# QK-normed attention and a layer-normed MLP on one core: first attention reordered, preparation moved between ScalarE, VectorE and GpSimd

## The chip, the cores and the metric

One core of one Trainium2 chip runs the whole kernel. The metric is the time of one execution in microseconds (us), as the device reports it; lower is better. The engines are TensorE (PE, with its weight loads shown as PEld), VectorE (DVE), ScalarE (ACT), GpSimd (POOL) and SyncE (SP, which here only issues DMAs). A line such as L789 is a line of the kernel before.

## The reference

Inputs are `q`, `k`, `v` of shape (8 batches, 12 heads, 448 positions, 64), the gains `g_q`, `g_k` (64), `g_ln` (768), and the MLP weights `w_ch1` (768 x 3072) and `w_ch2` (3072 x 768). All are float32, and so is the output (8, 448, 768).

```python
def rmsnorm(x, g):
    rms = np.sqrt(np.mean(x * x, axis=-1, keepdims=True) + 1e-06)
    return x / rms * g
q_n, k_n = rmsnorm(q, g_q), rmsnorm(k, g_k)
attn = softmax(q_n @ k_n.T / sqrt(64))          # over the keys
x = (attn @ v), heads side by side              # (8, 448, 768)
xn = (x - mean) / sqrt(var + 1e-06) * g_ln
out = x + relu(xn @ w_ch1) @ w_ch2
```

## The kernel before

**Units and pairs.** The 12 heads of a batch are 6 pairs, so there are 48 pairs, numbered 0 to 47. Loading and normalizing is done by units (`UNITS`, L22): batch 0 has units 0 and 1 with one pair each and units 2 and 3 with two pairs each (pairs 2, 3 and 4, 5); each later batch has three units of two pairs, so unit 4 is pairs 6 and 7, unit 5 is 8 and 9, unit 6 is 10 and 11, unit 7 is 12 and 13, unit 8 is 14 and 15. A pair has seven tiles of 128 keys: six of its own heads and one (i = 6) that takes the last 64 keys of both heads.

**Preparing a unit** is a set of small steps, each with a letter (`pieces`, L229 to L347). `b` takes the tiles. `a` and `c` square keys and queries (L257, ACT), `d` and `e` sum the squares over 64 columns (L260, DVE), `g` (or `gq`, `gk`) takes the reciprocal roots (L263, L264, ACT). `i` multiplies the keys by both gains (L274), `j` rounds them to 16 bits, the high part (L280 POOL or L282 ACT), `k` subtracts to get the low part (L285, DVE). `l` scales the queries (L82, DVE), `m` duplicates them beside the low and high keys (L321). `z` copies the values to 16 bits (L327, L333, POOL). The squares are written where the 16-bit tiles (`khl`, `qn`) will stand, so a high part waits for the sum that reads the squares. Which engine does a step for which unit is set by lists: `DVE_KG` for `i`, `POOL_HI` for `j`, `POOL_DUP` for `m`, and `ACT_Q`, by pair, for the copy of the transposed queries.

**Transposing.** Up to unit 6, PE transposes keys and queries pair by pair: `K` (`trans_k`, L363 and L366, copied out by DVE at L368) and `Q` (`trans_q`, L377 and L380, copied out by ACT at L383 or by DVE at L385). From unit 7 on (`DMA_UNIT`), SP issues transposing DMAs: steps `x` (keys, L301), `y` (queries, L307) and `Y` (the last 64 queries, the "left" ones, L313).

**Attention.** `S p.i` is the score product of a tile and its exponential: PE at L400 (or L406, L410, L411 for the seventh tile), then ACT at L416 with the key's norm as scale. `V p.i` multiplies the exponentials with the values (L453, L455); after the seventh, DVE evacuates the pair, divided by the sum (L468 to L475). Two PSUM banks take scores.

**MLP.** `T` takes statistics of finished pairs (L635, DVE), `A` aggregates them (L650), `N` normalizes a tile of 128 positions (L656), `X` transposes it (for batch 0 with PE at L692, copied by ACT at L696 and L698 or by DVE at L700; for later batches with SP's transposing DMAs, L682), `R` takes the root. For batch 0, `U` does the first three column blocks of the up product tile by tile (L936), then `first_mlp` does the other 21 blocks (L712, rectified by ACT at L715) and the down products (L722, added by DVE at L749). Later batches go by `mlp_group`, which forms the down product from seven block products in place of eight; its sums of weights (`weight_sums`, L755) are made by DVE near the end of batch 0's MLP.

**What sets the order.** Every engine works through its own instructions in the order in which they are written down. Up to the start of batch 0's MLP that order is the list `ORDER`, written out by hand: S, V, K, Q, T and the steps named above, with the unit or pair behind the letter. `H` and `J` are filler products and filler transposes on PE, so many as the number says. `L` loads a unit, `W` a third of the first weight matrix (POOL's queue), `G` and `G2` load and scale the layer norm's gain. Afterwards `attention` makes a list of steps for all later pairs, seven per pair, with what falls due at each: `EARLY` spreads the steps of units 5 to 9, `TRANS_AT` sets the steps for `x`, `y`, `Y`, `W2_AT` those for the second weight matrix (L610, POOL's queue; the second time POOL first waits for unit 7's transposed keys, L607). A step that stands in `ORDER` already is left out. `run_rest` mixes this list into the MLP of the batch before: after each chunk of MLP work it takes as many steps as its share. `TAIL` is the number of pieces of 960 ns of MLP work that are to be left when the steps are through; after that the norm of the next batch follows, one item per chunk.

**Loads.** SP issues most loads. Keys and queries of units have a ring of three buffers (`p_in`, tag "kq"); `RING` is the order in which they get them, and a buffer is loaded again when its low part (`k`) or scaled queries (`l`) are done. Some loads have a home of their own (`home`, L192) in memory that isn't yet in use: `hS`, which later takes the MLP's activations, and `free`, which later takes sums of weights.

## Time and profile before

| | |
|---|---|
| Median of 3 runs | 588.28 us (586.68 to 588.32) |
| The profiled execution | 588.25 us |
| Its span in the trace, first to last instruction | 586.6 us |
| Around the span | 1.65 us |
| Granted TensorE clock, mean | 0.999 |

Times in a trace are counted from the span's start. In the views, a row of a stretch of time gives start, duration, engine, line, operation, what it writes and reads, how many instructions were merged, and in brackets how long the engine had been idle before and who ended that. "SPq" and "POOLq" are the queues of the engines that issue DMAs. A time at which a row starts serves as its name in the text.

### The profile page before, as it was taken

What the parts mean: (1) busy time and instruction counts of PE and PEld (TensorE: products, weight loads), DVE (VectorE), ACT (ScalarE), POOL (GpSimd) and SP (SyncE); (2) the same over time, 40 slices, a digit from 0 to 9 for tenths busy, and PEclk for the clock granted to TensorE, in tenths of its full rate; (3) what the DMA queues carried; (4) which work ended last, traced back from release to release, by engine and by line L of the source; (5) the groups of instructions that cost most, each with busy time, mean ns of one, the idle gap of its engine ahead of it and who ended that gap; (6) DMA issues with size and microseconds to landing.
All of it is one profiled execution on the core that took longest, in us unless ns stands there. A gap on an engine that the chain in (4) does not pass through costs nothing.

```text
span 586.6 us, 13638 instructions
## 1 busy us (share of the span) xinstructions
PE 561.6 (96%) x5438; PEld 412.5 (70%) x5438; DVE 378.3 (64%) x831; ACT 378.9 (65%) x693; POOL 178.8 (30%) x200
## 2 busy tenths in 40 slices
PE   6777999999999999999999999999999999999996
PEld 5555566667677867777687767777777777777784
DVE  5898666697667586855757576864756733663424
ACT  5987888448785688647787488737787477323130
POOL 2945335303240520653141511643241410020000
PEclk9999999999999999999999999999999999999999
DMA  8999999969762786968753697959743490040201
GB/s 215 262 217 230 187 185 180 176 157 137 127 113 49 180 125 146 121 159 106 138 92 56 178 131 142 126 143 119 145 62 65 123 105 1 1 108 2 83 1 56
DMA packets 178328, 72.58 MB, mean 124 GB/s; under 512 B 138212, under 2 KB 173220, under 8 KB 178260
## 3 DMA queue, kind: packets, MB, share of 16 engines
q1 hardware_dynamic: 133876, 52.52, 44.0%
q0 software_dynamic: 43440, 18.52, 25.7%
q8 instruction: 43, 0.70, 0.5%
q10 hardware_dynamic: 944, 0.62, 0.5%
q14 instruction: 25, 0.20, 0.1%
HBM read 52.76 MB, written 11.01 MB: 109 GB/s over the span
## 4 chain that ended last, share of the span: by engine, by line
PE 77%; DVE 7%; ACT 3%; DMA 3%; issue 1%; SPq 1%; DVEq 0%; ACTq 0%
PE psH L789 32%; PE psP L812 27%; PE psS L400 7%; PE oA L453 4%; PE psH L712 3%; DMA q<-in_q_dram 2%; PE oB L455 1%; ACT E L416 1%; PE psS L406 1%; DVE stat L635 1%; DVE w2s L755 1%; DVE ssq L260 1%; ACT khl L257 1%; DVE xn L656 1%; DVE x L470 1%
## 5 line engine op out<-in xcount | busy, mean ns | idle before, releaser
L416 ACT ACTIVATE E<-psS,rr_all 128x448 f16<-128x448 f32 x336 | 203.7, 635 | 39.4 <-PE psS L400 33.7
L789 PE MATMUL psH<-xnT,w 128*128 128x256 f16 (+1 forms) x2016 | 225.8, 261 | 1.3 <-DVE x L749 1.3
L789 PEld LDWEIGHTS <-w 128*128 128x128 f16 x2016 | 172.6, 98 | 25.5 <-issue 6.4
L792 ACT ACTIVATE hS<-psH 128x512 f16<-128x512 f32 x150 | 90.1, 601 | 98.4 <-PE psH L789 94.0
L812 PEld LDWEIGHTS <-hS 128*128 128x128 f16 x1080 | 100.0, 98 | 57.5 <-issue 1.1
L812 PE MATMUL psP<-w,hS 128*128 128x384 f16 x672 | 126.8, 326 | 0.0
L400 PE MATMUL psS<-qU,kU 128*128 128x448 f16 x288 | 100.9, 352 | 7.3 <-ACT E L416 4.5
L453 PEld LDWEIGHTS <-E 128*128 128x128 f16 x1008 | 70.5, 98 | 35.6 <-issue 3.7
L274 POOL TENSOR_TENSOR k<-k,gprod 128x896 f32<-128x896 f32 x19 | 40.5, 2132 | 158.2 <-ACT khl L257 131.8
L795 DVE TENSOR_TENSOR hS<-hS 128x512 f16<-128x512 f16 (+1 forms) x119 | 56.8, 484 | 22.3 <-ACT hS L792 20.8
L812 PE MATMUL psP<-w2s,hS 128*128 128x384 f16 (+1 forms) x408 | 69.9, 321 | 0.0
L453 PE MATMUL oA<-v,E 128*128 128x65 f16 x864 | 66.4, 193 | 1.0 <-POOL v L327 0.6
L749 DVE SCALAR_TENSOR_TENSOR x<-psP,rs_all,x 128x384 f32<-128x384 f32 x60 | 36.4, 617 | 41.9 <-PE psP L812 41.2
L455 PE MATMUL oB<-v,E 128*128 128x65 f16 x288 | 51.7, 193 | 0.2
L823 POOL TENSOR_TENSOR x<-x,hS 128x384 f32<-128x384 f32 x21 | 23.5, 1128 | 83.5 <-ACT hS L891 82.9
L215 POOL DMA_DIRECT2D v<-in_v_dram x54 | 41.4, 777 | 9.0 <-PE oB L455 8.0
L468 DVE RECIPROCAL rec_all<-oA 128x6 f32<-128x6 f32 x48 | 9.2, 192 | 47.5 <-PE oA L453 47.4
L285 DVE TENSOR_TENSOR khl<-k,khl 128x896 f16<-128x896 f32 x19 | 20.8, 1094 | 29.3 <-ACT khl L282 29.2
L400 PEld LDWEIGHTS <-kU 128*128 128x128 f16 x288 | 28.0, 98 | 14.5 <-issue 3.5
L891 ACT ACTIVATE hS<-hS,rs_all 128x384 f32<-128x384 f32 x27 | 14.6, 605 | 33.1 <-DVE hS L795 33.1
L455 PEld LDWEIGHTS <-E 128*128 128x128 f16 x336 | 32.4, 97 | 0.2 <-DVE xl L475 0.2
L260 DVE TENSOR_REDUCE ssq<-khl 128x14 f32<-128x896 f32 (+1 forms) x24 | 25.5, 1063 | 10.1 <-ACT khl L257 9.2
(141 smaller groups left out, 610.0 us busy)
## 6 DMA issues: line engine op xcount, KB each, us to landing
k<-in_k_dram SPq DMA_DIRECT2D x19, 384.0 KB, 3.8
q<-in_q_dram SPq DMA_DIRECT2D x19, 384.0 KB, 4.3
out_dram<-x SPq DMA_DIRECT2D x14, 384.0 KB, 2.9
w<-in_moe_w_ch_dram POOLq DMA_DIRECT2D x3, 1536.0 KB, 15.7
v<-in_v_dram POOLq DMA_DIRECT2D x54, 64.0 KB, 4.6
out_dram<-x POOLq DMA_DIRECT2D x9, 384.0 KB, 2.7
w<-in_moe_w_ch_dram POOLq DMA_DIRECT2D x1, 2304.0 KB, 22.4
w<-in_moe_w_ch_dram POOLq DMA_DIRECT2D x2, 1152.0 KB, 14.3
```

The costliest lines, as they stand in the source:

```text
L215: nc.gpsimd.dma_start(out[:, :, j, 0:D], main[:, :, j])
L260: nc.vector.tensor_reduce(out=c["ssq"][:, n], in_=c["sq", n], axis=AX.X, op=ALU.add)
L274: (nc.vector if u in DVE_KG else nc.gpsimd).tensor_tensor(out=c["t"][1], in0=c["t"][1], in1=sh.gprod.unsqueeze(1).broadcast_to([128, g, D] ...
L400: nc.tensor.matmul(ps[0][:, 0:S], c["main"][:, ts(i, 128)], c["q"][:, ts(h, S)], start=True, stop=True)
L416: nc.scalar.activation(out=o, in_=x[:, 0:S], func=AFT.Exp, scale=self.units[u][3][:, g:g + 1], bias=EXP_BIAS)
L453: nc.tensor.matmul(oA[:, t, cs], E[:, ts(t, 128)], rhs, start=(i == 0 and t == 0), stop=(i == 6 and t == 2))
L455: nc.tensor.matmul(oB[:, cs], E[:, 320:448], rhs, start=(i == 0), stop=(i == 6))
L749: self.nc.vector.scalar_tensor_tensor(out=x, in0=ps, scalar=self.rs[:, b, t:t + 1], in1=x, op0=ALU.mult, op1=ALU.add)
L789: nc.tensor.matmul(ps[:, i], sh.w1[:, dc, ts(f + i, 128)], self.xnT[:, dc, 256 - N:256], start=(i == 0 and dc == 0), stop=(i == k - 1 and ...
L792: nc.scalar.activation(out=hT[:, f:f + k], in_=ps, func=AFT.Relu)
L795: nc.vector.tensor_tensor(out=out, in0=a, in1=c, op=op)
L812: nc.tensor.matmul(bank[x][:, c], a[:, f], w[:, f, c], start=(start and f == 0), stop=(stop and f == HALF - 1))
```

## The change

It has these parts.

1. **`ORDER`** is another permutation. It now holds `b`, `a`, `c`, `d`, `e` and `i` of unit 6 too (before, these fell due in the later list). Statistics of pairs 3 and 4 (`T3`, `T4`) stand among the score products of pair 5, where before they stood behind its last value product with `T5`; unit 5's query sum `e5` stands ahead of the third transposed tile `X2`; pair 7's query transposes `Q7` stand ahead of the first up products `U0`; unit 0's root of keys `gk0` and unit 2's steps stand earlier. There are 32 filler transposes in place of 24, and as many filler products (76).
2. **Engines.** Squares of unit 2's keys, unit 4's queries and unit 6's queries go from ACT to POOL, as a product (`POOL_SQUARE`). Low parts of units 5 and 6 go from DVE to POOL (`POOL_LO`). The gain product of unit 1 goes from DVE to POOL and that of unit 6 from POOL to DVE (`DVE_KG`). The high part of unit 6 goes from ACT to POOL. Duplicates of units 1 and 2 go from POOL to DVE, those of units 3, 5 and 6 from DVE to POOL. Transposed queries of pairs 2, 4 and 5 are copied by ACT in place of DVE, those of pair 1 by DVE in place of ACT.
3. **Unit 4's queries** are loaded into spare columns of `hS` and leave the ring, in which unit 6's keys and queries then come one place earlier. The lookup that loads a ring buffer again is written for that.
4. **`TRANS_AT`** of unit 8: the left queries' transposes (`Y`) come at step 91 in place of 86. On SP they then stand behind the two transposes of batch 1's first normalized tiles and four stores of batch 0's output, where before they stood ahead of all these.
5. **`TAIL`** of batch 0 is 11 in place of 12.
6. The two small tiles of sums and roots (`ssq`, `rt`) are taken at a unit's first sum and no longer at `b`.

```diff
@@ -25,7 +25,8 @@
 PAIR_UNIT = [(u, w) for u, (_, _, m) in enumerate(UNITS) for w in range(m)]
 UNIT_PAIR = [PAIR_UNIT.index((u, 0)) for u in range(len(UNITS))]
 EXP_BIAS = -4.0
-DVE_KG, POOL_HI, POOL_DUP, ACT_Q = (0, 1), (1, 2, 3, 4, 5), (1, 2, 4), (0, 1)
+DVE_KG, POOL_HI, POOL_DUP, ACT_Q = (0, 6), (1, 2, 3, 4, 5, 6), (3, 4, 5, 6), (0, 2, 4, 5)
+POOL_SQUARE, POOL_LO = ((2, 1), (4, 0), (6, 0)), (5, 6)
 
 
 
@@ -33,21 +34,21 @@
 
 
 ORDER = """
-H12 b0 a0 c0 L4 i0 H24 j0 e0 k0 gq0 l0 b1 m0 a1 c1 K0 Q0 H10 d0 G gk0 S0.0 S0.1 H5 d1 e1 L5 i1
-g1 j1 l1 k1 m1 z0 b2 a2 S0.2 d2 c2 S0.3 H16 S0.4 K1 V0.0 e2 i2 S0.5 Q1 g2 l2 S0.6 S1.0 H5 j2
-V0.1 S1.1 S1.2 H4 m2 b3 V0.2 a3 V0.3 k2 c3 S1.3 J16 K2 V0.4 S1.4 z2 V0.5 Q2 S1.5 V0.6 V1.0 i3 W0
-d3 e3 S1.6 V1.1 V1.2 S2.0 j3 T0 V1.3 S2.1 S2.2 Q3 V1.4 S2.3 K3 S2.4 V1.5 V1.6 S2.5 g3 z3 S2.6
-V2.0 S3.0 S3.1 V2.1 k3 S3.2 b4 S3.3 V2.2 l3 a4 V2.3 m3 S3.4 V2.4 K4 S3.5 Q4 V2.5 V2.6 S3.6 Q5
-S4.0 V3.0 S4.1 V3.1 i4 V3.2 d4 T1 K5 V3.3 W1 c4 V3.4 V3.5 S4.2 S4.3 V3.6 S4.4 S4.5 W2 e4 V4.0
-V4.1 j4 S4.6 S5.0 k4 S5.1 g4 V4.2 l4 S5.2 V4.3 V4.4 V4.5 S5.3 J4 K6 V4.6 z4 V5.0 S5.4 m4 b5 V5.1
-G2 S5.5 L6 V5.2 S5.6 V5.3 V5.4 V5.5 Q6 a5 i5 V5.6 T3 T4 S6.0 S6.1 S6.2 S6.3 T5 S6.4 A V6.0 V6.1
-N0 V6.2 N1 V6.3 S6.5 S6.6 d5 V6.4 J4 X0 X1 U0 N2 R Q7 X2 c5 e5 j5 g5 k5 l5 z5 U1 U2 V6.5 M m5
-V6.6 L7 L8k K7
+b0 H12 a0 L4 c0 i0 e0 j0 H24 b1 gq0 d0 k0 l0 a1 m0 K0 G gk0 i1 H10 L5 c1 Q0 d1 j1 S0.0 b2 S0.1
+H5 a2 e1 g1 S0.2 c2 S0.3 k1 l1 z0 d2 e2 m1 K1 S0.4 i2 H16 S0.5 S0.6 Q1 g2 H5 J8 b3 l2 j2 k2 c3
+V0.0 S1.0 z2 S1.1 S1.2 V1.0 J8 a3 m2 H4 V0.1 z3 S1.3 K2 S1.4 V0.2 Q2 V0.3 V0.4 d3 S1.5 V0.5 V0.6
+S2.0 S1.6 V1.1 V1.2 S2.1 e3 W0 i3 K3 V2.0 S2.2 V2.1 S2.3 Q3 j3 T0 S2.4 k3 V1.3 g3 V1.4 S2.5 S2.6
+l3 b4 V1.5 m3 c4 S3.0 S3.1 V2.2 S3.2 K4 a4 V1.6 S3.3 V2.3 S3.4 Q4 d4 V2.4 V2.5 V3.0 V3.1 V3.2
+V2.6 i4 S3.5 j4 J4 S3.6 V3.3 T1 K5 e4 k4 S4.0 W1 S4.1 S4.2 Q5 z4 b5 S4.3 V3.4 V4.0 V3.5 S4.4
+V4.1 V4.2 S4.5 W2 V4.3 S5.0 g4 V3.6 S4.6 S5.1 J4 V5.0 V4.4 G2 S5.2 l4 T3 K6 V4.5 V5.1 V4.6 S5.3
+T4 V5.2 a5 L6 V5.3 S5.4 m4 Q6 i5 S5.5 V5.4 S5.6 V5.5 V5.6 T5 S6.0 S6.1 J4 S6.2 A V6.0 S6.3 V6.1
+N0 N1 S6.4 S6.5 J4 V6.2 X0 V6.3 d5 j5 N2 S6.6 V6.4 X1 z5 Q7 c5 V6.5 R U0 e5 U1 g5 X2 V6.6 M k5
+U2 K7 b6 L7 a6 L8k c6 i6 l5 m5 e6 d6
 """.split()
 DMA_UNIT = 7
 PE_SET = (DMA_UNIT + 1) % 2
 EARLY = {5: (42, 49), 6: (47, 56), 7: (61, 69), 8: (75, 83), 9: (89, 97)}
-TRANS_AT = {7: (70, 71, 73), 8: (84, 85, 86), 9: (100, 102, 104)}
+TRANS_AT = {7: (70, 71, 73), 8: (84, 85, 91), 9: (100, 102, 104)}
 NAMES = {8: ["bai", "d", "c", "e", "j", "k", "gz", "l", "m"],
          9: ["bai", "d", "c", "j", "k", "e", "gz", "l", "m"]}
 W2_AT = 47, 71
@@ -64,10 +65,10 @@
 RS_RATIO = 4.0
 HALF, HCOL = NFF // 2, DM // 2
 DOWN = 10
-TAIL = (12, 13, 17, 13, 17, 13, 19, 0)
+TAIL = (11, 13, 17, 13, 17, 13, 19, 0)
 FLAG_AT = (6, 30)
 E_RING = 9
-RING = [(u, n) for u in (4, 6, *range(8, len(UNITS))) for n in "kq"]
+RING = [(4, "k")] + [(u, n) for u in (6, *range(8, len(UNITS))) for n in "kq"]
 
 
 def _rsqrt(nc, out, a, t, eps, mul=1.0):
@@ -189,7 +190,7 @@
         b, hs, m = UNITS[u]
         eng = nc.sync
         hS = self.hS.rearrange("p f n -> p (f n)").bitcast(FP32)
-        home = {(4, 2): (hS, 0), (5, 0): (hS, 1920), (5, 1): (hS, 2816), (5, 2): (hS, 3712),
+        home = {(4, 0): (hS, 896), (4, 2): (hS, 0), (5, 0): (hS, 1920), (5, 1): (hS, 2816), (5, 2): (hS, 3712),
                 (6, 2): (self.free, 3840), (7, 0): (self.free, 0), (7, 1): (self.free, 896),
                 (7, 2): (self.free, 1792)}
         t = self.loads.setdefault(u, [None] * 3)
@@ -241,8 +242,6 @@
 
         def begin():
             c["t"] = self.loads.pop(u)
-            c["ssq"] = self.p_n.tile([128, 2, 14], FP32, tag="ssq", name="ssq", bufs=1)[:, :, 0:g]
-            c["rt"] = self.p_n.tile([128, 2, 14], FP32, tag="rt", name="rt", bufs=1)[:, :, 0:g]
             c["rb"] = self.p_n.tile([128, 2, 14], FP32, tag="rq", name="rr_all", bufs=6)[:, :, 0:g]
             c["r", 0], c["r", 1] = c["rb"][:, 0], c["rb"][:, 1]
             c["qn"], c["khl"] = self.qn[u % 2][:, 0:g], self.khl[u % 2][:, 0:g]
@@ -254,9 +253,15 @@
             if u == 0 and n == 1:
                 o = self.free[:, 5376:5376 + g * D]
             c["sq", n] = o.rearrange("p (g d) -> p g d", d=D)
-            nc.scalar.activation(c["sq", n], c["t"][n], AFT.Square)
+            if (u, n) in POOL_SQUARE:
+                nc.gpsimd.tensor_tensor(out=c["sq", n], in0=c["t"][n], in1=c["t"][n], op=ALU.mult)
+            else:
+                nc.scalar.activation(c["sq", n], c["t"][n], AFT.Square)
 
         def total(n):
+            if "ssq" not in c:
+                for x in ("ssq", "rt"):
+                    c[x] = self.p_n.tile([128, 2, 14], FP32, tag=x, name=x, bufs=1)[:, :, 0:g]
             nc.vector.tensor_reduce(out=c["ssq"][:, n], in_=c["sq", n], axis=AX.X, op=ALU.add)
 
         def root(n=slice(0, 2)):
@@ -282,8 +287,8 @@
                 nc.scalar.activation(c["khl"][:, :, 0], c["t"][1], AFT.Identity)
 
         def klo():
-            nc.vector.tensor_tensor(out=c["khl"][:, :, 1], in0=c["t"][1],
-                                    in1=c["khl"][:, :, 0], op=ALU.subtract)
+            (nc.gpsimd if u in POOL_LO else nc.vector).tensor_tensor(
+                out=c["khl"][:, :, 1], in0=c["t"][1], in1=c["khl"][:, :, 0], op=ALU.subtract)
 
         def qn():
             if u < DMA_UNIT:
@@ -555,7 +560,8 @@
                 todo.setdefault(at, []).extend(
                     self.prep_ops(u)[y] for y in names if y + str(u) not in done)
                 for y in set(names) & set("kl"):
-                    i = RING.index((u, "qk"[y == "k"])) + 3 if u != 5 and u != 7 else nu * 2
+                    x = u, "qk"[y == "k"]
+                    i = RING.index(x) + 3 if x in RING else nu * 2
                     if i < len(RING):
                         todo.setdefault(at + (LOAD_AT[y == "l"] if u not in EARLY else 1), []).append(
                             lambda x=RING[i]: self.load_unit(x[0], ("qk".index(x[1]),)))
```

## The prediction

> **What bounds the kernel now.** I read the page's span and slices first, then busy time by stretch, then each engine in order of time.
>
> ```profile
> span 586.6 us, 13638 instructions
> ...
> PE   6777999999999999999999999999999999999996
> ...
> DVE  5898666697667586855757576864756733663424
> ACT  5987888448785688647787488737787477323130
> POOL 2945335303240520653141511643241410020000
> ```
>
> TensorE (PE) has work in nine tenths or more of every slice but the first four (14.7 us each) and the last. So whatever is to be won lies in the first 60 us, or in single short stops behind them. PE's own work is the same in both kernels but for eight filler transposes: every microsecond by which PE reaches its full rate sooner shortens the whole, and time of other engines off that path is worth nothing.
>
> ```profile
> 15.00:30.00 15.00, 11.30 (x148) 7.96 (x148) 12.09 (x19) 14.11 (x27) 14.12 (x16) 1.00 0.94 258
> 30.00:45.00 15.00, 11.84 (x160) 8.06 (x159) 14.50 (x28) 13.43 (x25) 7.26 (x9) 1.00 1.11 217
> 45.00:60.00 15.00, 11.65 (x160) 8.66 (x157) 13.41 (x36) 10.24 (x21) 6.70 (x6) 1.00 1.07 227
> ...
> 120.00:135.00 15.00, 13.66 (x134) 11.00 (x133) 14.68 (x27) 8.26 (x17) 0.00 (x0) 1.00 0.53 152
> ```
>
> The columns are start and end, length, busy us and count of PE, weight loads, DVE, ACT, POOL, then granted clock, DMA share, GB/s. From 15 to 45 us ACT is the bound (27.54 of 30 us busy, 2.46 idle), with DVE full in the second half. From 45 to 60 it is DVE (13.41), while ACT falls to 10.24: batch 0's attention ends and its MLP waits for the layer norm. At 120 there is one stop more. PE in order of time names the stops:
>
> ```profile
> 20.99 1.06 PE L530 MATMUL tr<-id 128*128 128x128 f16 x16
> 23.05 0.23 PE L363 MATMUL tr<-id,khl 128*128 128x128 f16 x1 [1.00 <-DVE khl L285]
> ...
> 42.65 0.23 PE L363 MATMUL tr<-id,khl 128*128 128x128 f16 x1 [0.64 <-DVE khl L285]
> ...
> 58.46 2.60 PE L712 MATMUL psH<-w2s,w 128*128 128x384 f16 x15
> 62.41 0.36 PE L400 MATMUL psS<-qU,kU 128*128 128x448 f16 x1 [1.35 <-DVE kU L368]
> ...
> 79.19 0.35 PE L400 MATMUL psS<-qU,kU 128*128 128x448 f16 x1 [0.28 <-ACT E L416]
> ...
> 123.03 1.47 PE L789 MATMUL psH<-xnT,w 128*128 128x256 f16 x12 [1.34 <-DVE x L749]
> ```
>
> Two waits for low parts of keys, one for the copy of pair 7's keys, a small one for ACT, one ahead of batch 1's MLP. From 62.41 on PE runs at full rate, so 62.41 is the point to move.
>
> **The change until batch 0's last exponential.** The prices on ACT, then DVE in order of time:
>
> ```profile
> 13.87 0.93 ACT L257 ACTIVATE khl<-w2s 128x896 f32<-128x896 f32 x1
> ...
> 17.77 0.90 ACT L383 COPY qU<-psQ 128x896 f16<-128x896 f16 x1
> ...
> 23.96 5.47 ACT L416 ACTIVATE E<-psS,rr_all 128x448 f16<-128x448 f32 x9 [0.58 <-PE psS L400]
> ...
> 43.79 1.89 ACT L416 ACTIVATE E<-psS,rr_all 128x448 f16<-128x448 f32 x3 [0.63 <-PE psS L400]
> ```
>
> ```profile
> 37.62 1.07 DVE L635 BATCH_NORM_STATS2 stat<-x 128x6 f32<-128x256 f32 x3
> ...
> 46.35 0.19 DVE L468 RECIPROCAL rec_all<-oA 128x6 f32<-128x6 f32 x1
> ...
> 47.67 2.24 DVE L635 BATCH_NORM_STATS2 stat<-x 128x6 f32<-128x256 f32 x9
> ...
> 54.70 0.62 DVE L385 COPY qU<-tr 128x896 f16<-128x896 f16 x1 [0.53 <-PE tr L380]
> 55.92 0.56 DVE L700 COPY w2s<-tr 128x768 f16<-128x768 f16 x1 [0.59 <-PE tr L692]
> 56.39 1.08 DVE L260 TENSOR_REDUCE ssq<-qn 128x14 f32<-128x896 f32 x1
> 57.38 1.08 DVE L285 TENSOR_TENSOR khl<-hS,khl 128x896 f16<-128x896 f32 x1
> 58.38 1.09 DVE L82 SCALAR_TENSOR_TENSOR qn<-hS,rr_all 128x896 f16<-128x896 f32 x1
> ...
> 61.70 0.66 DVE L368 COPY kU<-tr 128x960 f16<-128x960 f16 x1
> ```
>
> Up to batch 0's 42nd exponential ACT loses the squares of unit 2's keys and unit 4's queries, but unit 5's key square moves ahead of that point: one square less, -0.93. Query copies of pairs 2, 4 and 5 come to ACT and pair 1's leaves: two more, +1.80. So ACT has 0.87 **more** to do. Against it stand its 2.46 us of idleness. Two of its waits (0.58 and 0.63, together 1.21) follow PE's two stops for low parts (23.05, 42.65), and both low parts come sooner: POOL does unit 1's gain product itself instead of waiting for DVE, so its queue starts earlier, and DVE is rid of two query copies (0.62 each) and that product. Unit 0's key sum now stands ahead of its low part on DVE, before the first exponential; a sum of twice the size takes 1.08, so at most 0.5, and I take 0.4. If only those two waits go: +0.87 - 1.21 + 0.4 = +0.1. If all idle time goes: +0.87 - 2.46 = -1.6. If none: +1.3. DVE, the other full engine here, is relieved, so I lean to the good side: **-0.5**, ends -1.6 and +1.3.
>
> The eight fillers (1.06 / 16 each, 0.5 in all) stand where PE waits anyway: 0, at worst 0.5.
>
> **From there to full rate.** Pair 5's result is evacuated at 46.35. Then come nine statistics, the norm and its transposes; the copy of the third transposed tile (55.92 to 56.48) lets the third part of the up product go, and the MLP begins at 58.46. In the new order T3 and T4 stand before the last score products, so three of the nine statistics stay, 128 columns wide. The six narrow ones share 2.24 - 1.07, so three cost 0.6: -1.64. Unit 5's query sum moves ahead of the third copy: +1.08. Pair 7's query transposes move ahead of the first up products, so PE and DVE no longer wait for each other there: -0.53 and -0.59. Together **-1.68**, and the MLP begins at 56.8.
>
> Behind the third copy DVE did a sum, a low part and normed queries (56.39 to 59.47), small ones and an evacuation until 61.70, and only then pair 7's key copy. Now the low part and a duplicate are POOL's, the sum is paid above and the normed queries come behind the key copy. Left in front are the small ones and the evacuation, at most 61.70 - 59.47 = 2.23, so the copy ends near 56.48 - 1.68 + 2.23 + 0.66 = 57.7. PE gets there with its 15 products at 58.46 - 1.68 + 2.60 = 59.4. PE is the later one, so the stop goes: **-1.35**, and next late is PE itself. Both together -3.0; ends -1.0 if new POOL work drags the chain, -4.0 if the sums find holes.
>
> Unit 6's query square and high part leave ACT, its gain product goes to DVE, its low part to POOL. All that is off the path, but for ACT's share in the stop at 79.19: **-0.3**, ends 0 and -0.7.
>
> **POOL, which covers all this.**
>
> ```profile
> 17.36 2.08 POOL L274 TENSOR_TENSOR w2s<-w2s,gprod 128x896 f32<-128x896 f32 x1
> 19.50 1.67 POOL L280 CAST khl<-w2s 128x896 f16<-128x896 f32 x1
> ...
> 27.59 0.93 POOL L280 CAST khl<-w2s 128x896 f16<-128x896 f32 x1 [0.34 <-PE oB L455]
> ...
> 35.48 1.72 POOL L601 DMA_DIRECT2D w<-in_moe_w_ch_dram  x2
> ```
>
> ```profile
> w<-in_moe_w_ch_dram POOLq DMA_DIRECT2D x3, 1536.0 KB, 15.7
> ```
>
> The trace has no square and no low part on POOL. Nearest is the gain product, two inputs of the same size, 2.08, which I take (ends 0.93, the cast, and twice 2.08). POOL gains three squares, two low parts, a half-size product, a high part and two duplicates more than it loses: about 14 us over the first 65, of which it is idle more than half. Behind the duplicate for unit 3, which waits for DVE's normed queries, there now queue unit 4's query square, gain product and high part, and then the second and third load of the first weight matrix. If the second is issued 3 to 5 us later than 35.48, it lands at 54 to 56. It is wanted five column blocks behind the MLP's start, after 60. Cost 0; without that cover a microsecond for each by which it lands later. SP gains: unit 4's queries have a place of their own, so unit 6's no longer wait for a ring buffer, and what stands behind them (unit 6's values, unit 7) is issued earlier. The same bytes compete sooner; 0.
>
> One row shows DVE and POOL in each other's way:
>
> ```profile
> 21.20 1.79 DVE L285 TENSOR_TENSOR khl<-w2s,khl 128x896 f16<-128x896 f32 x1 [0.82 <-POOL khl L280]
> ```
>
> 1.79 beside a busy POOL, against 1.08 at 57.38; POOL's cast took 1.67 beside DVE, against 0.93. The sum has no more of it than that, and for this reason the first term is -0.5 and not -1.6.
>
> The Trainium skill, page "SBUF — State Buffer", section "Who interferes with whom", says that a DVE instruction with two SBUF inputs and a GpSimd instruction that reads SBUF lock each other out for the whole instruction. The rows just shown agree: 0.71 more on one, 0.74 on the other. By this rule the change is dearer than its own durations; rival 3 gives its time.
>
> **The stop at 123.** SP, DVE, and the landing of the transposed norm:
>
> ```profile
> 115.52 2.51 SPq L313 DMA_TRANSPOSE qU<-qn  x2
> 118.13 0.52 SPq L947 DMA_DIRECT2D out_dram<-x  x1
> 118.75 2.58 SPq L682 DMA_TRANSPOSE xnT<-xn  x2
> ```
>
> ```profile
> 113.50 1.88 DVE L656 SCALAR_TENSOR_TENSOR xn<-x,stat,gln 128x768 f16<-128x768 f32 x2
> ```
>
> ```profile
> DMA to landing us min/median/max: 2.7/2.7/2.7
> ```
>
> The norm is ready at 115.38, but SP issues unit 8's left queries first (2.51). The second norm transpose, issued near 120.1, lands 2.7 later, at 122.8, just before PE's 123.03. (The DVE instruction that the view names frees a bank that the third up product needs, not the first.) With the left queries behind, the landing is at 120.3, before PE's last down product ends (123.03 - 1.34 = 121.7). The shorter TAIL ends attention one 960 ns piece later, so the norm is ready at 116.3, about when SP is free. The stop goes: **-1.3**, ends 0 and -1.34. Unit 8's left queries then land some 8 us later than before, at about 128. They are wanted by its first scores, which come behind the six of pair 13 that begin after 124: cost 0.
>
> **Sum.** -0.5 - 3.0 - 0.3 - 1.3 = -5.1. The profiled execution took 588.25 us (span 586.6, and 1.65 around it); the median of the runs is 588.28, the same. 588.25 - 5.1 = 583.15, given as **583.2**. Ends: -1.6 - 4.0 - 0.7 - 1.3 = -7.6, so 580.6; +1.3 - 1.0 + 0.5 = +0.8, so 589.0.
>
> **Rivals.**
> 1. *ACT keeps the first stage.* It has 0.87 more to do and none of its waits goes: +1.3. The stretch behind gives -2.0, the norm's transposes -1.3: 586.2. For it: ACT is busy 14.11 of 15. Against: its two larger waits hang on low parts that come sooner.
> 2. *Every hole closes*: the good ends of the first two terms with the other two, -7.2, 581.0. Against it: DVE has work for nearly the whole time itself.
> 3. *Slower: DVE and POOL lock each other out.* Place: DVE from 18 to 58 us. Twelve of its instructions there have both inputs in SBUF (low parts of units 2 to 4, normed queries of units 2 to 5, the norm's four pieces, unit 6's product), and POOL is now busy for most of that time. Price 0.71 each, as at 21.20. From the eighth hit on the chain (5.7) it ends slower than before; ten cost 7.1 and give 590.2. For it: the row at 21.20, from the stretch in which POOL was busy 14.12 of 15. Against: a hit counts only while DVE sets the pace, and from 15 to 45 that is mostly ACT.
>
> That the change doesn't do what it says has no weight: the built order holds each of these moves.
>
> **Chances.** Forecast (every step in sign, 581 to 585.5) 0.55; rival 1 and mixes with it 0.2, half of that faster by over 0.3%; rival 2 0.1; rival 3 0.15. About 0.3% (1.8 us) is what a measurement of this kernel can tell from no change, so the edge is at 586.5. Faster: 0.55 + 0.1 + 0.1 = 0.75; same 0.1; slower 0.15. The range leaves out rival 3 and half of rival 2: 580.8 to 588.6.
>
> **What would show it.** PE's wait of 1.35 for pair 7's key copy gone, and the score product at 62.41 here at 58.5 to 59.5; three statistics, not nine, behind the last evacuation; no stop ahead of batch 1's first up product, with the norm's transposes directly behind unit 8's main queries on SP; POOL nearly full from 10 to 45. Wrong if pair 5's evacuation comes after 47, if DVE's two-input rows lengthen to 1.8 in numbers, if PE waits for a weight load in the first MLP, or if the norm lands after PE's last down product all the same.

## The result, and the profile after

The kernel after takes **585.6 us** (median of 16 runs, 584.9 to 587.71), the kernel before 588.63 beside it (median of 16, lowest 586.68; one of the 16 took 2051.58 us, of which no trace was kept, and the median of the other 15 is 588.45). The ratio, without that one, is 0.9951, with a 95% interval of 0.9937 to 0.9966: faster by 0.5%, some 2.9 us. The forecast was 583.2, so the sign and the range hold, and the time is 2.4 us above the forecast. The profiled execution of after took 586.28 us with a span of 584.7.

The page of after, span and slices, to be laid beside the five lines of before:

```profile
span 584.7 us, 13655 instructions
...
PE   6888999999999999999999999999999999999996
...
DVE  6989567799657566845667585854757634663424
ACT  4997887458784769557786588737787477323130
POOL 5885635303430710553240520643141410020000
```

TensorE's first four slices go from 6777 to 6888, and GpSimd's from 2945 to 5885. The same four stretches as before, with the same columns (busy us and count of PE, weight loads, DVE, ACT, POOL, then clock, DMA share, GB/s):

```profile
15.00:30.00 15.00, 12.73 (x165) 9.46 (x164) 14.06 (x20) 14.27 (x27) 12.36 (x14) 1.00 1.07 268
30.00:45.00 15.00, 12.52 (x173) 8.80 (x172) 13.26 (x30) 14.39 (x27) 12.36 (x12) 1.00 1.12 234
45.00:60.00 15.00, 13.44 (x166) 9.87 (x164) 14.54 (x37) 11.89 (x25) 7.81 (x7) 1.00 1.12 236
120.00:135.00 15.00, 14.21 (x145) 11.33 (x143) 14.88 (x26) 11.43 (x21) 2.09 (x1) 1.00 0.47 117
```

PE gains 3.9 us of work in the first three rows (12.73 + 12.52 + 13.44 against 11.30 + 11.84 + 11.65). ScalarE is now busy 28.66 of 30 us from 15 to 45, and in the last row VectorE has 0.12 us of 15 left. TensorE in order of time, at the places that the prediction named:

```profile
58.47 0.35 PE L405 MATMUL psS<-qU,kU 128*128 128x448 f16 x1
...
63.24 0.22 PE L382 MATMUL tr<-id,qn 128*128 128x128 f16 x1 [0.34 <-DVE kU L373]
...
76.23 0.35 PE L405 MATMUL psS<-qU,kU 128*128 128x448 f16 x1 [0.28 <-ACT E L421]
...
118.57 1.47 PE L795 MATMUL psH<-xnT,w 128*128 128x256 f16 x12
...
132.07 0.27 PE L458 MATMUL oA<-v,E 128*128 128x65 f16 x3 [0.72 <-DVE x L475]
...
220.15 0.35 PE L405 MATMUL psS<-qU,kU 128*128 128x448 f16 x1 [1.01 <-ACT E L421]
```

The wait of 1.35 us at 62.41 and that of 1.34 at 123.03 are gone. ScalarE's small one of 0.28 (then at 79.19) is still there, and there are three new ones: at 63.24 behind VectorE's key copy, behind VectorE at 132 and behind ScalarE at 220. (The bracket gives the idle time by the profile, in which the end of a product is modelled. Where the text below has another size for a stop, it is the distance between two starts less the usual distance of such products. By this measure the stop at 132 is 0.89, with 0.22 more at the next product.) The same events in both traces, read from the timelines, show where the lead comes from and where it goes:

| event | before | after | lead | forecast |
|---|---|---|---|---|
| first exponential | 12.46 | 13.39 | +0.93 | +0.4 |
| fifteenth exponential | 25.91 | 25.88 | -0.04 | |
| pair 5's evacuation | 46.35 | 46.62 | +0.27 | -0.5 |
| the score product at 62.41 | 62.41 | 58.47 | -3.94 | -3.5 |
| pair 7's evacuation | 77.91 | 74.95 | -2.96 | -3.8 |
| batch 1's first up product | 123.03 | 118.57 | -4.46 | -5.1 |
| pair 13's evacuation | 143.05 | 139.72 | -3.32 | -5.1 |
| pair 21's | 226.45 | 223.99 | -2.46 | -5.1 |
| pair 33's | 359.80 | 358.11 | -1.69 | -5.1 |
| last product | 580.74 | 579.04 | -1.70 | -5.1 |

(A negative lead is earlier. Of the 3.94, 0.5 is only order: before had issued 15 up products by then, after 12, at 0.16 us each.) The sum came within 0.6 us of the forecast where its last term ends, at 118.57. Then 2.8 us were given back in three places, and nothing between them: from pair 13 to pair 19 the lead is 3.32 to 3.33 at every pair. The experiments ask what took the lead back, and what made it.

### The profile page after: what moved, and what is told of

The parts are those of the page before. It is cut to its first block, busy times and chain, and to the rows that moved or that the text cites. A ratio compares the mean times of both kernels' runs of the same rounds, so it can differ in the third digit from the quotient of the medians.

```text
span 584.7 us, 13655 instructions
## 1 busy us (share of the span) xinstructions
PE 563.6 (96%) x5446; PEld 414.6 (71%) x5446; DVE 379.6 (65%) x826; ACT 376.9 (64%) x691; POOL 190.7 (33%) x207
## 4 chain that ended last, share of the span: by engine, by line
PE 70%; DMA 10%; DVE 8%; ACT 5%; SPq 2%; issue 2%; POOL 1%; DVEq 0%; ACTq 0%; POOLq 0%
PE psH L795 30%; PE psP L818 27%; PE psS L405 6%; PE oA L458 4%; DMA q<-in_q_dram 3%; ACT E L421 3%; DMA v<-in_v_dram 2%; DMA w2s<-in_k_dram 2%; SPq L154 2%; DVE w2s L761 1%; PE oB L460 1%; PE psS L411 1%; DVE ssq L265 1%; DVE qn L83 1%; DMA kU<-khl 1%
## 5 line engine op out<-in xcount | busy, mean ns | idle before, releaser
L818 PE MATMUL psP<-w,hS 128*128 128x384 f16 x672 | 126.8, 326 | 0.0
L279 POOL TENSOR_TENSOR k<-k,gprod 128x896 f32<-128x896 f32 x18 | 38.4, 2132 | 149.6 <-ACT khl L259 133.1
L290 DVE TENSOR_TENSOR khl<-k,khl 128x896 f16<-128x896 f32 x18 | 19.6, 1089 | 28.8 <-ACT khl L287 27.6
```

What stands on the lines that cost most here:

```text
L279: (nc.vector if u in DVE_KG else nc.gpsimd).tensor_tensor(out=c["t"][1], in0=c["t"][1], in1=sh.gprod.unsqueeze(1).broadcast_to([128, g, D] ...
L818: nc.tensor.matmul(bank[x][:, c], a[:, f], w[:, f, c], start=(start and f == 0), stop=(stop and f == HALF - 1))
```

## Experiments

Theory A: the first stage and the stop ahead of batch 1 gave nearly what was forecast. TensorE then had to wait for two others that have no time to spare: VectorE with its weight differences, and a query load that stands on SP behind a chain of transposes. The rivals are in the expectations. "Earlier" and "later" are against after where no other kernel is named; ratios are against before, which was measured again on each of the three chips used (medians 588.62 to 589.21). After's own ratio is 0.9951 (0.9937 to 0.9966). Steps of 1 us or less are not separated by the intervals; for these the traces carry the argument.

### Where the lead goes: VectorE from 113 to 132

**The left queries alone, in the kernel before.**

```diff
-TRANS_AT = {7: (70, 71, 73), 8: (84, 85, 86), 9: (100, 102, 104)}
+TRANS_AT = {7: (70, 71, 73), 8: (84, 85, 91), 9: (100, 102, 104)}
```

> The kernel before with one edit: the left queries of unit 8 go on SP behind the norm transposes of batch 1 (list index 86 becomes 91). Theory A (the stop ahead of batch 1's first up product goes, and VectorE, which is 14.68 of 15 us busy from 120 to 135, then becomes late at pair 12's evacuation): the stop of 1.5 us at 123.03 shrinks to about 0.2, batch 1's first up product starts at 121.7 in place of 123.03, but pair 12's evacuation stays within 0.4 us of its old 133.80, TensorE's product behind it waits for VectorE some 0.8 us, and the kernel ends 0.3 to 0.6 us earlier (588.0 beside 588.5). Rival B (VectorE has room; the gain is kept): evacuation and end are both 1.3 us earlier (587.2). Rival C (the landing of the norm transposes was never set by the left queries): nothing moves.

587.91 us (median of 12), ratio 0.9978 (0.9964 to 0.9993). The up product starts at 121.43, 1.60 earlier than before's 123.03, and its stop is gone. Pair 12's evacuation is only 0.35 earlier; a stop of 0.45 stands ahead of the product behind it, and pair 13's is 0.91 earlier. So TensorE won 1.6 and VectorE's queue took back 0.7. This is theory A, with a price a little below its own, and rivals B and C fall. The query loads (below) took the rest in this trace, while the median is 0.9 us ahead of before's.

**The same edit undone in after** (91 becomes 86 again).

> The kernel after with the left queries of unit 8 back ahead of the norm transposes (91 becomes 86). Theory A: TensorE stops again about 1.3 us ahead of batch 1's first up product (118.57 becomes about 119.9), but the stop of 1.1 us at 132 behind VectorE goes, since TensorE comes there later and VectorE's queue is the same; the end is 0 to 0.4 us later than after's (585.6 to 586.0). Rival B (the stop at 132 has another cause and stays): both stops, 1.3 us later than after (586.9).

587.11 us (median of 12), ratio 0.9969 (0.9946 to 0.9991). A miss: the up product is only 0.27 later than after's, at 118.84. SP's rows of this execution (start, duration, kind, target and source, count):

```profile
101.44 5.43 SPq L306 DMA_TRANSPOSE kU<-khl  x1
106.98 4.30 SPq L312 DMA_TRANSPOSE qU<-qn  x3
111.33 2.52 SPq L318 DMA_TRANSPOSE qU<-qn  x2
...
114.57 2.55 SPq L688 DMA_TRANSPOSE xnT<-xn  x2
```

and those of after:

```profile
101.69 6.72 SPq L306 DMA_TRANSPOSE kU<-khl  x1
108.51 4.77 SPq L312 DMA_TRANSPOSE qU<-qn  x3
...
114.00 2.57 SPq L688 DMA_TRANSPOSE xnT<-xn  x2
```

The keys took 5.43 here and 6.72 there, the queries 4.30 and 4.77, and with that most of the 2.52 for the left queries was made up. The key transposes of this place take from 5.43 to 7.83 us in the executions of this study. In this execution, then, the left queries cost only what of their 2.52 SP could not make up. The stop at 132 did not go either: it is 0.51 by its row, in place of 0.72.

The runs show a cost that this trace does not. Four of the twelve took 588.22 to 589.15 us at a mean granted clock of 0.995 or 0.996; the other eight took 585.21 to 587.54. No run of after is above 587.71 or below a clock of 0.997. In the kernel before, the same move of the left queries left no run above 588.71 or below 0.998, while the unchanged kernel beside it went up to 592.35, at 0.996. So the later place seems to pay most where the wait is long enough to cost clock, as in the next trace; no trace of those four runs was kept.

**What a long wait there costs.** A second trace of the kernel before (a single run):

> The kernel before, unchanged, for a second trace of it. If the waits of ScalarE for query loads near 221 and 356 differ between executions (the first trace of before has 0.31 us there and none, while before with late left queries has 1.14 and 0.45), this execution shows 0.3 to 1.2 us of TensorE stop at one place or both, and every other stop as in the first trace, within 0.1 us; the span is then 586.6 to 588. If the stops belong to the kernels that reach those places early, it shows 0.31 and none again, and 586.6.

591.31 us, and both kinds of stop are larger; that the one at 123 would grow was not expected. SP, then TensorE, then a stretch of the table by time:

```profile
103.50 7.77 SPq L301 DMA_TRANSPOSE kU<-khl  x1
...
116.28 2.51 SPq L313 DMA_TRANSPOSE qU<-qn  x2
...
119.53 2.59 SPq L682 DMA_TRANSPOSE xnT<-xn  x2
```

```profile
123.83 2.71 PE L789 MATMUL psH<-xnT,w 128*128 128x256 f16 x12 [2.63 <-DVE w2s L755]
```

```profile
124.00:127.00 3.00, 3.00 (x16) 2.02 (x15) 1.35 (x2) 0.42 (x1) 0.00 (x0) 0.54 0.63 239
```

The keys took 7.77, TensorE waited 2.63 us, and then its granted clock was 0.54 from 124 to 127: twelve up products took 2.71 in place of 1.47. Against the first trace the up product is 0.79 later and batch 1's first down product 2.21: the clock cost 1.4 us on top of the wait. Up to there this execution had been 0.5 us ahead. A stop of 1.12 at 224 followed, behind a query load, where the first trace has 0.31; at 356 there is none in either. So the first trace of before was one of the better executions of that kernel, and in after the same spread of SP falls on a shorter queue. This fits the medians, which differ by more (2.9 us) than the two profiled executions (1.97).

**VectorE's weight differences earlier.** Twelve differences of the down weights (0.75 us each) stand between 113 and 126, ahead of pair 12's evacuation, and ahead of them VectorE has a wait, the hole of the expectations. In after:

```profile
105.94 0.62 DVE L755 SCALAR_TENSOR_TENSOR x<-psC,rs_all,x 128x384 f32<-128x384 f32 x1 [4.04 <-PE psC L728]
...
131.04 0.18 DVE L473 RECIPROCAL rec_all<-oA 128x6 f32<-128x6 f32 x1
```

First the four that need no other, four chunks of MLP work earlier:

```diff
-            ops += [lambda a=a: sub(*a) for a in ((t1, b12, b11), (t2, b22, t1), (t4, b21, t2))]
+            ops[c:c] = [lambda a=(t1, b12, b11): sub(*a)]
+            ops += [lambda a=a: sub(*a) for a in ((t2, b22, t1), (t4, b21, t2))]
...
-                if (left < 9 if b == 0 else b == 1) and ops:
+                if (left < 9 or 10 < left < 15 if b == 0 else b == 1) and ops:
```

> The kernel after with the first four of the twelve differences of down weights (second column half minus first, of the upper rows, 0.75 us each) issued four chunks earlier, where VectorE waits 4.04 us at 105.94 for a down product, and the other eight as before behind the sixteenth down chunk. Theory A (VectorE is the bound from 113 to 132): its 3 us leave that stretch, pair 12's evacuation comes about 1.1 us earlier (131.04 becomes about 130), the TensorE stop of 0.89 + 0.22 us at 131 to 132 goes, and all after it is 1.1 us earlier: 584.5 beside after's 585.6. Rival B (the stop at 132 hangs on something else, such as the locked difference of 2.23 us at 132.38 or the gains on GpSimd): no change, 585.6. Rival C (the early differences delay the norm of batch 1 or the evacuation of pair 9 by waiting for the down weights' landing at 98.48): later by up to 2 us.

585.67 us (median of 8), ratio 0.9944 (0.9923 to 0.9965): no change. The stop at 132 is gone, but the last two of the four came behind VectorE's wait. The later of them ran beside the gains on GpSimd and took 1.65, pair 11's evacuation and the norm were 1.75 later, and two stops of 0.52 and 0.69 took the place of the old one; pair 13's evacuation moved by 0.06. Theory A was not tried by it, since only two of the four stood in the hole. Then all four in two chunks, with the list put in order as above:

```diff
-                if (left < 9 if b == 0 else b == 1) and ops:
-                    ops.pop(0)()
+                for _ in range(left < 9 or 2 * (12 < left < 15) if b == 0 else b == 1):
+                    if ops:
+                        ops.pop(0)()
```

> The kernel after with the four first differences of down weights issued in two chunks earlier still, so that they stand in VectorE's wait of 4.04 us ahead of the down product's sum at 105.94 and ahead of the gains on GpSimd at 106.88. Theory A (VectorE's order from 113 to 132 is what TensorE waits for): pair 11's evacuation stays at 107.8 and the norm at 111.0, unlike with the differences in four chunks; VectorE has 2 to 3 us less to do before pair 12's evacuation, which comes at 128.5 to 129.5, no TensorE stop over 0.3 us is left between 119 and 134, and pair 13's evacuation is 1.1 us ahead of after's 139.72. Of that, the waits for query loads near 219 and 353 take back a part that differs between executions; the end is 584.6 to 585.6. Rival B: another engine's stop takes its place at 121 to 130 (as the 0.52 and 0.69 us with four chunks) and pair 13's evacuation stays within 0.3 us of 139.72.

**584.61 us** (median of 6), ratio 0.9928 (0.991 to 0.9946). VectorE of this kernel:

```profile
101.69 2.76 DVE L761 TENSOR_TENSOR w2s<-w 128x1152 f16<-128x1152 f16 x4
...
128.91 0.19 DVE L473 RECIPROCAL rec_all<-oA 128x6 f32<-128x6 f32 x1
```

The four stand in the wait, the norm comes when it did, pair 12's evacuation 2.13 earlier. No stop is left between 119 and 134, and pair 13's evacuation is 1.26 earlier, of which 0.13 is an earlier start. What is left, 1.13, is the stop of 0.89 + 0.22 in full: VectorE's order of work was what TensorE waited for.

**The shorter TAIL undone** (11 becomes 12).

> The kernel after with the attention steps of batch 1 spread to the old end (the change moved them one step earlier: 11 becomes 12). Theory A: the norm of batch 1 comes about 1 us earlier or later at most and the stop at 132 stays within 0.5 us of its size, so 585.6 within 0.6. Rival (the earlier norm and with it the earlier attention steps are what overload VectorE): the stop at 132 shrinks below 0.4 and the end is 0.7 us earlier.

585.76 us (median of 8), ratio 0.9951 (0.993 to 0.9971). The stop at 132 is 0.42, but ScalarE's at 76 is 0.94 in place of 0.45; pair 13's evacuation is 0.1 later. So the stop's size moved and the place where VectorE lets TensorE go did not. The profiled execution, at 583.86 the shortest of the eight, reaches the last product 0.9 earlier than after's, and all of that lies behind pair 13, at the query load of the next section. The median is not earlier, so no worth of the shorter TAIL is shown either way.

### Where the lead goes: the query loads near 219 and 353

In after, ScalarE's wait, and SP ahead of it:

```profile
218.62 0.95 ACT L259 ACTIVATE qn<-q 128x896 f32<-128x896 f32 x1 [2.32 <-DMA q<-in_q_dram]
```

```profile
208.67 1.22 SPq L688 DMA_TRANSPOSE xnT<-xn  x1
209.94 3.35 SPq L318 DMA_TRANSPOSE qU<-qn  x2
213.39 0.53 SPq L146 DMA_DIRECT2D q<-in_q_dram  x1
```

The square holds up the exponentials behind it, and they hold up TensorE (the 1.01 at 220.15). In before, the last two of these rows are:

```profile
212.72 2.52 SPq L313 DMA_TRANSPOSE qU<-qn  x2
215.33 1.52 SPq L145 DMA_DIRECT2D q<-in_q_dram  x1
```

The chain of transposes does start with the lead: its first one, of the norm, is at 198.43 in after and at 201.76 in before, 3.33 earlier. But the same transposes took longer in this execution (the left queries 3.35 against 2.52), and the load is issued only 1.94 earlier. So this is not work that keeps a time of its own. TensorE loses 0.84 to 1.26 us at this spot in ten of the twelve traces in which SP has this order; the first trace of before lost 0.31, and after with the longer TAIL 0.24. Among the ten are the other two traces with before's first list and engines (1.12 and 1.14). So most of the 0.86 given back here looks like a stop that the first trace of before happened to escape.

Near 353 the loss is 0.35 to 1.14 in all of these but the two traces of before, which have none. There too the chain starts with the lead (333.01 against 335.47). One norm transpose in it then takes 2.05 to 2.51 us in after and its variants, 1.22 in both traces of before and 1.91 in before with late left queries. Why was not tested.

First, every left query behind the load:

```diff
-        (12, "z"), (15, "x"), (16, "y"), (18, "Y"))
+        (12, "z"), (15, "x"), (16, "y"), (24, "Y"))
```

> The kernel after with the left queries of every unit from the tenth on transposed six attention steps later, which puts them on SP behind the next query and key loads in place of ahead of them. Theory Q (the stops of 1.18 us at 218 and 0.71 us at 353 are ScalarE's square of queries whose load was issued on SP only when the left transposes, 2.5 to 3.6 us, were through): the load is issued some 3 us earlier, ScalarE's wait for it of 2.32 us falls below 0.5, both stops go, and the kernel is about 1.5 us faster than after: 584.1. Rival D (the load is late because the DMA engines are busy then, whatever the order on SP): the stops stay. Rival E (the left transposes, now later, are late for the unit's own left scores): a new stop of 0.5 us or more in each batch, and slower than after by 1 to 5 us.

599.22 us (median of 5), ratio 1.0173 (1.0154 to 1.0192): slower, rival E. TensorE, then SP:

```profile
206.73 0.53 PE L405 MATMUL psS<-qU,kU 128*128 128x448 f16 x1 [4.56 <-DMA qU<-qn]
```

```profile
197.75 0.41 SPq L146 DMA_DIRECT2D k<-in_k_dram  x1
...
199.49 1.34 SPq L688 DMA_TRANSPOSE xnT<-xn  x1
200.88 2.56 SPq L318 DMA_TRANSPOSE qU<-qn  x2
```

and the waits of SP from 185 to 203:

```profile
SPq L146 <- DVE qn L326: 7.5, 1, 7.5
```

In two places the left queries went behind a key load that waits for its buffer (7.5 us here), and behind a norm transpose, and so the scores waited 4.56 us for them. From 207 to 210 the clock was 0.50. A second stop, of 5.57 us, ends at 349. Then the same swap for the two units alone that meet the late load, with the differences in the hole kept:

```diff
+LATE_Y = (12, 18)
...
-            plan = [(7 * (p - 4) + x, y) for x, y in PLAN]
+            plan = [(7 * (p - 4) + x + 3 * (y == "Y" and u in LATE_Y), y) for x, y in PLAN]
...
-                        todo.setdefault(at + (LOAD_AT[y == "l"] if u not in EARLY else 1), []).append(
+                        todo.setdefault(at + (LOAD_AT[y == "l" or u - 1 in LATE_Y] if u not in EARLY else 1), []).append(
```

> The kernel after with the first differences of down weights in VectorE's hole, and besides, for the twelfth and the eighteenth unit alone, the left queries three steps later and the next query load two steps earlier, which swaps just these on SP: the load is issued ahead of the left transposes, and the key load stays behind them. Theory Q (the stops near 217 and 352 are the query load's place on SP behind the left transposes): the load is issued at about 208.8 in place of 212.24, it lands 2 to 3.4 us earlier, ScalarE's wait goes below 0.5 us, both stops (0.99 and 0.57 us) go, and the kernel is 1 to 1.5 us faster than with the differences alone: 583.1 to 583.6. Rival D (the load's landing hangs on the DMA engines, not on its place): it lands within 1 us of before, and the end stays at 584.6. Rival E (the left transposes become late for their scores): a new stop near 222 to 230, and 584.6 or more.

**583.94 us** (median of 6), ratio 0.9912 (0.9885 to 0.994), the fastest of all. SP and ScalarE:

```profile
209.89 0.53 SPq L147 DMA_DIRECT2D q<-in_q_dram  x1
...
212.71 2.52 SPq L319 DMA_TRANSPOSE qU<-qn  x2
```

```profile
216.40 0.95 ACT L260 ACTIVATE qn<-q 128x896 f32<-128x896 f32 x1 [0.25 <-DMA qU<-qn]
```

The load is issued 3.5 us earlier, the square starts at 216.40 in place of 218.62, and neither stop is there. (The releaser named in the row is the profile's guess; no load is waited for any more.) Theory Q holds: what made the load late was its place in SP's order. The last product's lead over before is 4.10 us, and nothing of it is lost behind pair 13, where it is 3.58; after falls there from 3.32 to 1.70. (By the runs alone, this kernel and the one with the differences in the hole are not told apart.) In this execution the wait ahead of batch 1 had come back with 0.78 us, beside key transposes of 7.83.

### What makes the lead: the first stage

**T3 and T4 back behind pair 5's values.**

```diff
-S5.2 l4 T3 K6 V4.5 V5.1 V4.6 S5.3 T4 V5.2
+S5.2 l4 K6 V4.5 V5.1 V4.6 S5.3 V5.2
...
-V5.6 T5 S6.0
+V5.6 T3 T4 T5 S6.0
```

> The kernel after with the statistics of pairs 3 and 4 moved back behind the values of pair 5 (ahead of T5, as before). Theory A (the time until the first score product of unit 5's successor at full rate, 58.47 in after, hangs on VectorE's chain evacuation, statistics, norm, copies from 46.62 to 54.52): the chain gets 1.07 + 0.68 us back, the first norm starts at about 50.7 in place of 48.97, the third copy at 56.2 in place of 54.52, and the product at 60.0 in place of 58.47; the end is 1.6 us later than after's: 587.2. Rival B (the chain is not what sets it, but ScalarE's 49 exponentials, which end at 51.91): the product moves by less than 0.4 and the end stays at 585.6.

587.49 us (median of 10), ratio 0.9978 (0.9962 to 0.9994), 1.9 us above after's median. In the trace the norm starts at 50.42, 1.45 later; but the score product comes at 61.34, 2.87 later, and pair 7's evacuation is 2.36 later. The extra is the clock:

```profile
50.00:52.00 2.00, 0.77 (x10) 0.60 (x10) 2.00 (x7) 0.13 (x1) 0.00 (x0) 0.92 1.15 208
52.00:54.00 2.00, 2.00 (x21) 1.55 (x19) 2.00 (x3) 1.61 (x4) 0.40 (x1) 0.50 1.12 211
```

TensorE had little to do while VectorE worked off the statistics, and was then granted half its clock; between the norm and the first up product the delay grew from 1.45 to 2.70. Theory A holds, with a price above the forecast 1.68, and rival B falls. How often the clock falls there is open: the mean granted clock of the ten runs goes from 0.992 to 1.000, and this one had 0.995.

**Unit 1's gains back on VectorE** (0 and 6 become 0, 1 and 6).

> The kernel after with unit 1's gains back on VectorE as before (GpSimd keeps those of units 2 to 5). Theory L (the first exponential is 0.93 us late because GpSimd's gains at 9.00, 1.55 us, hold up VectorE's query copy at 9.60, 1.10 in place of 0.29 us): the copy takes 0.3 again, the first exponential starts at 12.6 in place of 13.39, the eighth 0.5 to 0.9 earlier than 20.32. What it gives at the end says where the first stage is bound: if ScalarE sets the pace from the first exponential on, all 49 exponentials and the product at 58.47 come 0.5 to 0.9 earlier (585.0); if the fifteenth exponential, which is level with before's already, takes it up, nothing comes of it (585.6). Rival K (unit 0's key sum, which now runs ahead, is what delays the first exponential): it stays at 13.0 or later.

586.11 us (median of 6), ratio 0.9952 (0.993 to 0.9975). VectorE's copy of unit 0's queries in after, and then in this kernel:

```profile
9.60 1.10 DVE L326 COPY qn<-qn 128x448 f16<-128x448 f16 x1
...
12.52 2.08 DVE L290 TENSOR_TENSOR khl<-w2s,khl 128x448 f16<-128x448 f32 x1 [0.21 <-POOL khl L285]
```

```profile
9.60 0.29 DVE L326 COPY qn<-qn 128x448 f16<-128x448 f16 x1
```

The gains on GpSimd (9.00, 1.55 us) held the copy up by 0.81. The first exponential is 1.30 earlier without them, at 12.09, but the copy is not all of that: six transposes of the queries on TensorE took 0.84 us in after's trace and 0.50 here. In six other traces that begin with after's own steps the copy is as slow as in after, the transposes as fast as here, and the first exponential comes at 12.58 to 13.00. The key sum is still ahead of it, so rival K falls. By the fifteenth exponential 0.34 is left of the 1.30, and at the last product 0.60; the runs show no gain (0.9952 against 0.9951). The hold-up is real and nearly free: something else sets the fifteenth.

**GpSimd's squares and low parts back** (the two lists emptied).

> The kernel after with the three squares (unit 2's keys, unit 4's and unit 6's queries) back on ScalarE and the low parts of units 5 and 6 back on VectorE. Theory M (the moves relieve ScalarE's first stage): three squares of 0.93 us on ScalarE ahead of the product at 58.47 put off the 42nd exponential's end from 46.18 by about 1 us and the product by 0.5 to 1.9; the end is 0.5 to 1.9 us later than after's (586.1 to 587.5). Rival L (what GpSimd's square takes from VectorE by holding it up, unit 1's low part at 12.52 for 2.08 in place of 0.61 us, costs as much as ScalarE saves): the low part takes 0.6 to 0.7 us, the eighth exponential is 0.5 to 0.9 us earlier than 20.32, and the end is within 0.5 of after's.

588.74 us (median of 10), ratio 0.9991 (0.9968 to 1.0013). The trace is 0.98 later at the last product, the score product 1.37. Unit 1's low part, the second row of the fence above, takes 0.62 in place of 2.08, and the eighth exponential is not earlier for it (20.45, 20.32 in after). The square of unit 2's keys on ScalarE costs 0.1 by the fifteenth exponential. That of unit 4's queries, behind it, costs its whole 0.93: the 29th and the 42nd are 0.93 later. So theory M holds in the trace, but only one of the three squares makes the difference, and rival L falls. The three differ, it seems, because ScalarE is full only from the fifteenth exponential to the 42nd, where it is busy 18.99 of 19.67 us in after. The runs of this kernel are further behind than its trace and theory M have it, by 1 us or more, which stays open.

**The old list with the new engines** (the whole first list of before).

> The kernel after with the first stage's list of before, so that only the engines of the pieces, unit 4's query load and the later left queries differ from before. Theory A (the list carries the gain of the first stage, above all the statistics of pairs 3 and 4 off VectorE's chain, which alone is worth 2.4 to 2.9 us; the moves between engines without it give little): the product at full rate is at 61.4 to 63, and the end 2 to 4 us later than after's: 587.6 to 589.6. Rival P (the moves between engines carry it): the product at 59 to 60.5 and the end at 586 to 587.

591.84 us (median of 10), ratio 1.0037 (1.0016 to 1.0058): **slower than before**. The score product comes at 63.88, later than theory A's 61.4 to 63; rival P falls. Here the hold-ups do count. TensorE from 18 to 24 us:

```profile
18.00:21.00 3.00, 0.87 (x9) 0.35 (x7) 2.98 (x5) 0.71 (x3) 2.94 (x3) 1.00 1.08 283
21.00:24.00 3.00, 2.87 (x32) 2.29 (x31) 2.88 (x3) 3.00 (x6) 1.98 (x4) 0.69 0.69 194
```

VectorE and GpSimd are both full from 18 to 21, ScalarE and TensorE starve (0.71 and 0.87 of 3), and the clock falls behind it. The fifteenth exponential is 2.64 later than in before. So the moves between engines, put into the old list, cost some 2 us; with the new list they are part of a gain of 3. They can't be priced apart from the list.

## Why the prediction was right, and where it was not

**Until batch 0's last exponential: -0.5 forecast, +0.27 measured.** ScalarE's idle time was recovered only in part, and I had taken two unlike stretches for one. From the first to the fifteenth exponential ScalarE does less (11.75 us busy against 12.63) and starts 0.93 later, of which 0.81 is the hold-up of the query copy and not the key sum that I charged. From there to the 42nd it has 1.57 us more to do (18.99 against 17.42) and recovers 1.04 of its idle 1.72. My +0.87 was the sum over both stretches. Both of the waits for low parts that the step names are gone, so of its own cases it came nearest to the one in which only these two go (+0.1), and not to the -0.5 to which I leaned.

**From there to full rate: -3.0 forecast, -3.7 measured** (-4.21, less the 0.5 of order). The statistics did what the step says: three are left behind the evacuation, the norm is 1.26 earlier than in before, the third copy 1.40, and pair 7's key copy ends at 57.75, ahead of TensorE. VectorE of after:

```profile
46.62 0.20 DVE L473 RECIPROCAL rec_all<-oA 128x6 f32<-128x6 f32 x1
...
47.97 0.68 DVE L641 BATCH_NORM_STATS2 stat<-x 128x6 f32<-128x128 f32 x3
...
48.97 2.03 DVE L662 SCALAR_TENSOR_TENSOR xn<-x,stat,gln 128x384 f16<-128x384 f32 x3
...
54.52 0.56 DVE L706 COPY w2s<-tr 128x768 f16<-128x768 f16 x1
...
57.09 0.66 DVE L373 COPY kU<-tr 128x960 f16<-128x960 f16 x1
57.85 1.79 DVE L279 TENSOR_TENSOR k<-k,gprod 128x896 f32<-128x896 f32 x1
...
62.55 0.64 DVE L373 COPY kU<-tr 128x960 f16<-128x960 f16 x1
```

Counted from pair 5's evacuation, the copy is 1.67 earlier than in before, where the step says 1.68. The MLP's first product (56.52 against 58.46) is 2.21 earlier, 0.5 more than the step has it, and the stop that went was 1.5 by the distance of the products, not 1.35. In the trace, putting T3 and T4 back costs more than the copy's share because TensorE's clock then falls, which before's own trace does not show there.

**ScalarE's stop at 79: -0.3 forecast, +0.5 measured.** The stop of 0.28 stayed (76.23), and a new one came at 63.24, 0.34 by its row and 0.5 against the usual distance of these instructions: pair 8's query transposes wait for the bank that pair 8's key copy frees, the last row above, and on VectorE this stands behind unit 6's gains (57.85, 1.79), unit 5's normed queries and unit 6's sums. By this order "All that is off the path" was wrong for the gains, which the change puts on VectorE; no run moved them alone.

**What was put at nothing** held: no stop behind a weight load, a filler or unit 8's left queries is in the trace of after. GpSimd was busy 24.72 of 30 us from 15 to 45, less full than I had it; a square there took 1.68 us, where I had taken 2.08.

**The stop at 123: -1.3 forecast, -1.50 measured.** Mechanism and size held: the norm's transposes stand directly behind the main queries on SP, and the stop is gone. The step took the row of one execution for a constant, though. In another one the wait is twice as long and takes the clock with it.

**The sum, and the step that failed.** The four terms give -4.46 at 118.57 against -5.1. What failed is the sentence on which the sum rests: "every microsecond by which PE reaches its full rate sooner shortens the whole". It is true from pair 13 to pair 19, to 0.01 us. It is not at 132, where VectorE's differences decide (1.1 us given back), nor at 219 and 353, where a query load behind SP's transposes does (0.86 and 0.77). The loss at 132 follows from the change. Of the one at 219 most looks like luck of the first trace of before, and at 353 it is open why a transpose took longer. The row 120:135 with VectorE at 14.68 of 15 us was among the prediction's rows by stretch, and I did not ask what a TensorE that comes there sooner would meet.

**Rival 3 (the lock) did not come.** From 18 to 58 us, the place that it names, only unit 6's gains (57.85) show the 1.79 of the hit at 21.20. The copy at 9.60 and the low part at 12.52, ahead of that place, were held up too; the copy cost 0.34 us at the fifteenth exponential, and without the low part's hold-up the eighth came no earlier. The Trainium skill, page "SBUF — State Buffer", section "Who interferes with whom", counts copies that run in a mode with two ports among those that can be locked as well, and the copy's 1.10 against 0.29 agrees; I had counted instructions with two inputs alone. With the old list the moves between engines did end slower than before, with VectorE and GpSimd both full from 18 to 21 us; how much of that is the lock was not separated.

## What to carry to other kernels

A lead won early is kept only up to the next place at which the leading engine waits for another one that has no time to spare: before summing up, go through the busy table for every later stretch in which another engine or a queue is full, and ask when its work could have begun. The two edits that kept the lead add no work at all: independent VectorE work put into an existing wait, and one load put ahead of transposes that nobody needs yet. Check such a swap unit by unit, since the same move applied to all units made the kernel some 13 us slower than after.

## What the hardware showed beside that

TensorE's granted clock fell in these traces without any long stop, behind stretches in which it had little to do. In three traces it was 0.50 for 3.4 us: from 123.4 to 126.8 in the second trace of before, from 51.7 to 55.1 with T3 and T4 moved back, and from 22.1 to 25.6 with the old list. The longest wait just before was 2.63, 1.24 and 2.13 us; one of 1.34 us in before left the clock at 1.00. The Trainium skill, page "TensorE: Matmul & The Clock Gate", section "What's actually happening", puts the fall behind an idle window of about 3.4 us. In the 3.4 us up to the fall TensorE was busy here for 1.25, 1.73 and 1.18 us (119.95 to 123.36, 48.25 to 51.65, 18.73 to 22.12), so it need not be idle for the whole of it. Where the edge lies is not settled: with unit 1's gains on VectorE a stretch of that length had 1.71 us of work (16.17 to 19.58), and the clock behind it stayed at 1.00.

The same key transposes on SP took 5.43 to 7.83 us in different executions of nearly the same program. What stands behind them on SP inherits that spread: in the two traces of before, 6.81 and 7.77 us go with waits of 1.34 and 2.63 us at 123.
